# A gated convolution–MLP kernel: the gate's weights loaded as one row, and a new order of all tasks

## The chip, the cores and the metric

The kernel runs on one core of a Trainium2 chip. The metric is device time in microseconds (us); lower is better. The engines of the core are TensorE (matrix products, PE in the profile), VectorE (DVE), ScalarE (ACT), GpSimd (POOL) and SyncE (SP), which here only issues transfers (DMAs).

## The reference, cut to what matters

One token matrix x (2048 × 640, bf16) goes through two branches, and a gate per token mixes them:

```python
g = _sigmoid((x * gate_w).sum(-1, keepdims=True))
a = _A_ref(x, A_k, A_v, A_shift_k, A_ssm_k, A_ssm_D)   # q * (long convolution of (short conv of k) * v)
b = _B_ref(x, B_w1, B_w2, B_w3, B_w4)                  # layernorm, w1, gelu, token shifts, w2, layernorm, w3, gelu, w4
return g * a + (1 - g) * b
```

Branch A's long convolution (length 2048, FFT of 4096) is done with products by small trigonometric matrices in stages. `gate_w` has 640 elements; the gate needs it twice: as columns that multiply the transposed, normalised x, and as its sum (because the layernorm's mean is subtracted afterwards).

## The kernel before, in words

The work is cut into 788 tasks. `build` declares them with their reads, writes and buffers. A task runs on one engine and issues a few instructions. The order is written out by hand in `ORDER`: a list of all task numbers, with a letter where a task may run on more than one engine (`a` ACT, `v` DVE, `p` POOL). `Plan.place` walks this list with rough durations to choose PSUM banks and to decide how many products of zeros (`t.fill`) are put ahead of a TensorE task to fill its expected waits in the first microseconds. Each engine then executes its own tasks strictly in the listed order, and waits when one is not ready. So an engine can be held up by one late task although later ones are ready, and SP, which issues nearly all DMAs, holds back every transfer behind one that waits.

PSUM has 8 banks: a `w1`, `w3` or gate product takes one, most others a pair; a bank is free again when ACT or DVE has copied it out.

Task names used below (the number after the point is the token block, block group or frequency block):

- `ldx`, `ldsk`, `ldk`, `ldv`, `ldw…`: loads. `cjz`, `ldCJ`, `cjb`, `cj`: the short convolution's taps; a strip of zeros on 128 partitions (`cjz`, ACT, L488) gets the taps in its first partition (`ldCJ`, L491), a product with ones spreads them over all partitions (`cjb`, L497), and `cj` copies them out.
- `sin`, `bm`: the trigonometric table (ACT, L471) and the DMA that spreads it into the block matrix of the first FFT stage (L481).
- `st1`, `rs1`, `nm1`, `tr1`, `ev1`, `evh`: first layernorm per block: statistics (DVE or ACT), their root (POOL), normalising, transposing on TensorE (L572), copying out (L387 on DVE, L385 on ACT); `evh` makes shifted copies of two blocks.
- `trh`, `evt`, `dfold`: transposing the long kernel (L805) and copying it out.
- `w1`, `g1`, `w2`, `x1`, `sq`: first half of branch B (L647 and L651, gelu L664, L673, L680, L685); `ve2`, `st2`, `nm2`, `dt2`, `w3`, `g2`, `w4`, `t2`: its second half (L767, L774, L781/L788, L796). `dt2` is a transposing DMA (L759).
- `kv0`–`kv3`: the short convolution on DVE (L825, L829, L833).
- `s1h`, `s1hr`, `s1x`, `s1xr`, `e1…`, `wF`: first FFT stage of the kernel (h) and of kv (x) (L858, L860), copied out and written to DRAM (L890). `rF`, `s2`, `e2`, `pa`/`pb`, `s3`, `e3`, `wG`: read back (L904), second stage (L912), products (L927), way back (L940), written out (L952). `rG`, `s4`, `yq`, `ad`, `ax`, `fo`, `st`: last stage (L966, L978), gate and sum (L984, L1011, L992, L998), store.
- `ldgw`, `sgm`, `sg`, `gate`, `gz`, `gtanh`, `gg`: the gate. `ldgw` (L503) loads `gate_w` with the partition as its fastest index, so that each element goes to its own place; `sgm` (L692) sums it over partitions with a product by ones; `sg` reduces that and copies the five columns 32 times (`GB`, L697).
- `fill`: the products of zeros (L254).

TensorE tasks have a mode by the shape of their products (full, or parts of the array in rows or columns); two neighbours of different mode cost a little extra.

The order ends the kernel with the `w4` products of blocks 12 to 15 and their `fo` on DVE.

Of the kernel before, what the change touches and what calls it, by code (L numbers as in the profile page):

```python
# [16 lines left out]
P = 128  # L17
D = 640
# [13 lines left out]
FILL_US = (0.43, 0.22)  # L32
# [4 lines left out]
14 4 5 0 9 1 8 7 10 29 30 12 28 16 71v 6 17 15 31 69a 46 2 81a 3 24 27 61v 70 72 22 25a 18 23a 20 82 59v 21a 26  # L37
19a 74v 44 73v 60 87v 79v 88 11 215 75 76v 401 405 77v 84a 216 80 63a 402v 62 406a 32 83v 68p 45 403 89v 64v 43
399 400v 404v 97a 85 91v 90 65 86a 67v 42 397 398v 92a 93 94v 66a 98 100v 41 36 407 127 13 33 105v 460 95a 466
129 128 96 47 99v 461a 103v 106 464 133 50 101 102v 78p 39 467a 465a 108v 130 104 35 468 411 49 469a 462 134 131  # L40
37 48 409 448 132 463a 149 107v 38 119v 456 449a 109 457a 135 454 450 34 150 120 110a 153 410 136 40 408 157 151
455a 51 451a 412 413 452 155 121v 158 471 152 414 415 416 122 137 417 140 138 52 154 56 156 159 160 470 453a
124a 141 146 143 147 144 123a 125 126v 111a 112 472 113a 115v 114 116v 458 478 148 479a 420 473a 145 162 163 139
165 166 474 168 55 459 227 476 475a 169 117 477a 118v 421 480 422 481a 484 485a 54 142 492 171 488 172 173 177
174 175 489a 217 221 179 222 423 228 178 419 424 425 426 57 490 493a 418 225v 486 176 482 193 223a 218 427 195
180 483 487a 491a 184 194 496 219 196 185 431 231a 504 190 181 505a 497a 500 191 182 229a 501a 201 53 430 432
224 202 502 494 498 433 499a 503a 199 197 187 200 198 495 167 434 188 508 509a 516 203 226 232 428 230 204 429
435 233 517a 241 161 514 234 510 512 242 239 253 506 507 511a 164 240 513a 58 206 515a 235 254 436 437 440 520
# [35 lines left out]
class Plan:  # L84
# [62 lines left out]
    def place(self, order):  # L147
# [8 lines left out]
        for i in order:  # L156
# [33 lines left out]
            else:  # L190
                d = t.dur
                if e == "PE":
# [3 lines left out]
                    if at < WARM:  # L196
                        d *= COLD
                        if self.kept is not None:
                            t.fill = int(0.85 * (at - max(free[e], 0.8)) / FILL_US[0])
# [153 lines left out]
def build(env, nc, io):  # L353
# [19 lines left out]
    def dma(name, nbytes, fn, issue=0.58, **kw):  # L373
        return add(name, "SP", issue, fn, nbytes=nbytes, **kw)
# [679 lines left out]
```

## Time and profile before

| what | value |
|---|---|
| median of 3 runs | 228.67 us (228.23 to 228.74) |
| the profiled execution's own time | 228.84 us |
| its span in the profile | 227.1 us |
| mean granted TensorE clock | 0.992 of full |
| busy: PE, DVE, ACT, POOL | 216.0, 191.2, 156.1, 44.1 us |
| DMA | 57.25 MB, mean 252 GB/s |

The profiled execution took 1.74 us more than its span, which lies ahead of and behind the first and last instruction that the profile shows. The page's busy time of PE counts the products of zeros too (L254, 29 of them, 10.5 us), so it is not all work. The chain of waits names, from the end backwards, what released each step; shares by line tell where the kernel's time is set.

### The profile page before, as it was taken

What the parts mean: (1) busy time and instruction counts of PE and PEld (TensorE: products, weight loads), DVE (VectorE), ACT (ScalarE), POOL (GpSimd) and SP (SyncE); (2) the same over time, 40 slices, a digit from 0 to 9 for tenths busy, and PEclk for the clock granted to TensorE, in tenths of its full rate; (3) what the DMA queues carried; (4) which work ended last, traced back from release to release, by engine and by line L of the source; (5) the groups of instructions that cost most, each with busy time, mean ns of one, the idle gap of its engine ahead of it and who ended that gap; (6) DMA issues with size and microseconds to landing.
All of it is one profiled execution on the core that took longest, in us unless ns stands there. A gap on an engine that the chain in (4) does not pass through costs nothing.

```text
span 227.1 us, 5043 instructions
## 1 busy us (share of the span) xinstructions
PE 216.0 (95%) x1994; PEld 104.9 (46%) x1994; DVE 191.2 (84%) x273; ACT 156.1 (69%) x224; POOL 44.1 (19%) x91
## 2 busy tenths in 40 slices
PE   7679899999999999999999999999989999999993
PEld 2258444456445444445543333344344554545552
DVE  8988889988999999998488889798987147998982
ACT  8889899899979999979459888888965014132000
POOL 8874237730380000031330000000000000000000
PEclk9799999999999999999999999999999999999999
DMA  5899999899947899968899997989996595898632
GB/s 153 216 293 338 234 282 292 244 323 302 341 147 242 180 306 343 291 237 219 203 357 358 250 320 188 288 314 345 197 190 217 153 406 182 235 301 240 207 92 58
DMA packets 41609, 57.25 MB, mean 252 GB/s; under 512 B 15985, under 2 KB 31602, under 8 KB 41586
## 3 DMA queue, kind: packets, MB, share of 16 engines
q1 hardware_dynamic: 41266, 56.61, 84.6%
q8 instruction: 15, 0.25, 0.5%
q10 hardware_dynamic: 320, 0.33, 0.5%
q14 instruction: 8, 0.07, 0.1%
HBM read 34.90 MB, written 18.35 MB: 235 GB/s over the span
## 4 chain that ended last, share of the span: by engine, by line
PE 76%; DMA 8%; DVE 6%; ACT 5%; SPq 3%; issue 1%; DVEq 0%
PE PS L767 19%; PE PS L781 18%; PE PS L673 9%; PE PS L647 6%; PE PS L788 6%; PE PS L912 5%; PE PS L940 4%; DMA x<-in_A_q_dram 4%; DMA SK<-in_A_ssm_k_dram 3%; PE PS L858 3%; SPq L380 2%; ACT FS L385 2%; PE PS L978 2%; PE PS L651 2%; DVE VC L829 2%; DVE VC L825 2%
## 5 line engine op out<-in xcount | busy, mean ns | idle before, releaser
L774 ACT ACTIVATE h2T<-PS 128x512 bf16<-128x512 f32 x48 | 28.1, 602 | 29.4 <-PE PS L767 28.6
L781 PE MATMUL PS<-W,h2T 128*128 128x512 bf16 (+1 forms) x288 | 40.3, 299 | 0.0
L385 ACT CAST FS<-PS 128x1024 bf16<-128x1024 f32 x38 | 37.0, 1025 | 2.6 <-PE PS L860 1.6
L767 PEld LDWEIGHTS <-W 128*128 128x128 bf16 x240 | 21.3, 98 | 31.0 <-issue 9.3
L781 PEld LDWEIGHTS <-h2T 128*128 128x128 bf16 x288 | 22.2, 98 | 19.2 <-issue 1.5
L385 ACT CAST XH<-PS 128x1024 bf16<-128x1024 f32 x23 | 22.9, 1014 | 9.0 <-PE PS L912 8.0
L767 PE MATMUL PS<-x1nT,W 128*128 128x512 bf16 x120 | 28.5, 380 | 0.0
L767 PE MATMUL PS<-XB,W 128*128 128x512 bf16 x120 | 28.3, 380 | 0.0
L927 DVE TENSOR_TENSOR PP<-XH 128x2048 bf16<-128x2048 bf16 x20 | 23.6, 1221 | 1.7 <-ACT XH L385 1.0
L825 DVE TENSOR_TENSOR VC<-K,VC 128x2560 bf16<-128x2560 bf16 x16 | 23.8, 1486 | 0.2
L673 PE MATMUL PS<-W,hsT 128*128 128x512 bf16 (+1 forms) x160 | 23.4, 299 | 0.3 <-DVE x L680 0.3
L387 DVE CAST XH<-PS 128x1024 bf16<-128x1024 f32 x17 | 20.5, 1220 | 3.2 <-PE PS L912 1.5
L796 DVE TENSOR_TENSOR x<-PS,x 128x640 bf16<-128x640 f32 x12 | 9.8, 823 | 13.3 <-PE PS L781 13.3
L647 PE MATMUL PS<-xnT,W 128*128 128x512 bf16 x80 | 19.2, 379 | 0.9 <-ACT hsT L664 0.9
L673 PEld LDWEIGHTS <-hsT 128*128 128x128 bf16 x160 | 13.0, 98 | 11.8 <-issue 0.5
L829 DVE TENSOR_TENSOR VC<-VC 128x2560 bf16<-128x2560 bf16 x12 | 17.9, 1488 | 0.4
L740 POOL TENSOR_TENSOR r<-v,MH 128x2 f32<-128x2 f32 x8 | 8.2, 1021 | 50.3 <-DVE v L735 47.7
L385 ACT CAST GS<-PS 128x1024 bf16<-128x1024 f32 x15 | 14.7, 1020 | 3.8 <-PE PS L940 3.8
L984 DVE SCALAR_TENSOR_TENSOR W<-PS,GG,QO 128x640 bf16<-128x640 f32 x16 | 13.6, 878 | 3.0 <-PE PS L978 3.0
L680 DVE SCALAR_TENSOR_TENSOR x<-PS,x 128x640 bf16<-128x640 f32 x16 | 12.8, 821 | 1.0 <-PE PS L673 1.0
L788 PE MATMUL PS<-W,h2T 128*128 128x512 bf16 (+1 forms) x96 | 13.4, 299 | 0.0
L912 PE MATMUL PS<-FX,TRIG 64*32 64x512 bf16 x320 | 12.7, 382 | 0.3 <-DVE GS L387 0.3
(111 smaller groups left out, 294.8 us busy)
## 6 DMA issues: line engine op xcount, KB each, us to landing
FH<-FS SPq DMA_DIRECT2D x8, 640.0 KB, 5.4
FXD<-FS SPq DMA_DIRECT2D x8, 640.0 KB, 4.7
FX<-FH SPq DMA_DIRECT2D x10, 512.0 KB, 5.1
FX<-FXD SPq DMA_DIRECT2D x10, 512.0 KB, 5.7
GX<-GD SPq DMA_DIRECT2D x8, 640.0 KB, 5.5
W<-in_B_w_dram SPq DMA_DIRECT2D x2, 1920.0 KB
GD<-GS SPq DMA_DIRECT2D x8, 480.0 KB, 3.3
x<-in_A_q_dram SPq DMA_DIRECT2D x16, 160.0 KB, 3.4
```

Of the source, the lines that this page charges most:

```text
L385: nc.scalar.copy(out=out, in_=in_)
L387: (nc.vector if t.on == "DVE" else nc.gpsimd).tensor_copy(out=out, in_=in_)
L647: nc.tensor.matmul(m[:, b, :], lhsT=W[:, 0, kb, 160 * fb:160 * fb + 128], rhs=rhs(kb, shifts[fb]), start=(kb == 0), stop=(kb == 4))
L673: nc.tensor.matmul(m[:, c0:c1], lhsT=env["hsT"][:, o.buf["hs"][0], fb, 128 * (s % 4):128 * (s % 4) + 128], rhs=env["W12"][:, 1, fb, c0:c1] ...
L767: nc.tensor.matmul(env.PS[:, t.buf["U"][0], :], lhsT=env["W3"][:, kb, 128 * fb:128 * fb + 128], rhs=env.nT(int(nP[-1]))[:, :, kb, :], star ...
L774: nc.scalar.activation(out=env["h2T"][:, o.buf["h2"][0], fb, :], in_=env.PS[:, t.buf["U"][0], :], func=ACT.Gelu_apprx_tanh)
L781: nc.tensor.matmul(m[:, c0:c1], lhsT=env["h2T"][:, o.buf["h2"][0], fb, 128 * (s % 4):128 * (s % 4) + 128], rhs=env["W4"][:, fb, c0:c1], st ...
L788: nc.tensor.matmul(env.PS[:, t.buf["U"][0], 0:c1 - c0], lhsT=env["h2T"][:, o.buf["h2"][0], fb, 128 * (s % 4):128 * (s % 4) + 128], rhs=env ...
L825: nc.vector.tensor_tensor(out=VC[:, o], in0=env["K"][:, a + 3 - j:a + 7 - j, :], in1=w, op=ALU.mult)
L829: nc.vector.tensor_tensor(out=VC[:, 1], in0=VC[:, 1], in1=VC[:, 2], op=ALU.add)
L912: nc.tensor.matmul(env.U(t.buf["U"][0])[32 * j:32 * j + 32, gp, :], lhsT=CRI()[64 * gp:64 * gp + 64, 32 * pc:32 * pc + 32], rhs=X[64 * gp: ...
L927: nc.vector.tensor_tensor(out=env["PP"][:, o.buf["PP"][0], a, :].rearrange("p (b c) -> p b c", b=2), in0=X.unsqueeze(1).broadcast_to([P, 2 ...
```

## The change

1. `ldgw` loads `gate_w` as one row of 1,280 bytes into the first partition of the same strip of zeros that holds the taps; the strip and `cjz` grow from 2,560 to 3,200 columns.
2. A new TensorE task `gwm` multiplies five pieces of that strip by one column of ones: each product gives one column of 128 weights. A new DVE task `gwc` copies the five columns to `GW`, and 32 times to `GB`. `sg` loses its copy.
3. The rule for products of zeros in the first 7.5 planned microseconds goes from 0.85 to 0.95 of an expected wait. In the program as built there are 33 products of zeros, 29 before: 19 stand ahead of the first product with data (12 before), 14 in later waits (17 before).
4. `ORDER` is replaced as a whole: every engine's sequence is different, and some tasks change engine.

```diff
-14 4 5 0 9 1 8 7 10 29 30 12 28 16 71v 6 17 15 31 69a 46 2 81a 3 24 27 61v 70 72 22 25a 18 23a 20 82 59v 21a 26
...
+5 14 32 4 0 80p 9 1 16 31 8 6 70p 30 2 7 10 83a 73v 15 12 61v 45 17 27 3 84 81v 74 28 71a 29 18 63v 86v 33 22 11
...
-                            t.fill = int(0.85 * (at - max(free[e], 0.8)) / FILL_US[0])
+                            t.fill = int(0.95 * (at - max(free[e], 0.8)) / FILL_US[0])
...
-    add("cjz", "ACT", 2.2, lambda t: nc.scalar.copy(out=env.early("CJR", [P, 4 * D], BF16).rearrange("p (a b) -> p a b", b=512),
-                                                    in_=env.early("FZ", [P, 512], BF16).unsqueeze(1).broadcast_to([P, 5, 512])),
-        use=[zeros], w=["CJR"], roles=("C0",))
+    add("cjz", "ACT", 2.7, lambda t: nc.scalar.copy(out=env.early("CJR", [P, 5 * D], BF16).rearrange("p (a b) -> p a b", b=400),
+                                                    in_=env.early("FZ", [P, 512], BF16)[:, 0:400].unsqueeze(1).broadcast_to([P, 8, 400])),
+        use=[zeros], w=["CJR", "GWR"], roles=("C0",))
...
-    dma("ldgw", 2048, lambda t: nc.sync.dma_start(out=env.sm("GW", [P, 5], BF16)[:],
-                                                  in_=io["gw"].rearrange("(t p) -> p t", p=P)), w=["GW"])
+    dma("ldgw", 1280, lambda t: nc.sync.dma_start(out=env.early("CJR", [P, 5 * D], BF16)[0:1, 4 * D:5 * D], in_=io["gw"].unsqueeze(0)),
+        w=["GWR"], roles=("C0",))
+
+    def gwm(t):
+        row = env.early("CJR", [P, 5 * D], BF16)
+        for kb in range(5):
+            nc.tensor.matmul(env.PS[:, t.buf["U"][0], kb:kb + 1], lhsT=row[:, 4 * D + 128 * kb:4 * D + 128 * kb + 128],
+                             rhs=env["ONE"][:, 0:1], start=True, stop=True)
+    tw = add("gwm", "PE", 0.3, gwm, r=["GWR", "c0"], use=[fill], acq=[ONE], mode="f", roles=("C0",))
+
+    def gwc(t):
+        m = env.PS[:, tw.buf["U"][0], 0:5]
+        nc.vector.tensor_copy(out=env.sm("GW", [P, 5], BF16)[:], in_=m)
+        nc.vector.tensor_copy(out=env.sm("GB", [P, 5, 32], BF16)[:], in_=m.unsqueeze(2).broadcast_to([P, 5, 32]))
+    add("gwc", "DVE", 0.4, gwc, use=[tw], rel=[(tw, "U")], w=["GW"])
...
     def sg(t):
         nc.vector.reduce_sum(out=env.sm("SG", [P, 1])[:], in_=env.PS[:, ts.buf["U"][0], 0:5], axis=mybir.AxisListType.X)
-        nc.vector.tensor_copy(out=env.sm("GB", [P, 5, 32], BF16)[:], in_=env.sm("GW", [P, 5], BF16).unsqueeze(2).broadcast_to([P, 5, 32]))
-    add("sg", "DVE", 0.35, sg, use=[ts], rel=[(ts, "U")], r=["GW"], w=["SG"])
+    add("sg", "DVE", 0.2, sg, use=[ts], rel=[(ts, "U")], r=["GW"], w=["SG"])
```

The new order, as far as the prediction speaks of it:

| stretch | before | after |
|---|---|---|
| DVE up to `evh.14` | `st1` ×6, `nm1` ×5, `ev1.0`, `evh.0`, `sg`, `evt` ×3 | `st1` ×6, `gwc`, `nm1` ×4, `ev1.2`, `ev1.0`, `sg`, `evt` ×3 |
| ACT up to its first `e1h` (both with `sin` in it: before behind the four `cj`, after ahead of them) | 3 `nm1`, `ev1.2`, `ev1.14`, gelu of `w1.0.0` among others | 4 `nm1`, `evh.0`, `ev1.14`, the same gelu; otherwise the same tasks |
| PE from the first `w1` to the first `w2` | 10 `w1`, 8 `s1h`, 2 `s1hr`, `tr1.6`, `tr1.8` | 10 `w1`, 7 `s1h`, 1 `s1hr`, `tr1.4`, `tr1.6`, `tr1.8` |
| DVE up to `kv0.v` (the last of kv) | | one `nm1`, one `nm2`, `ve2.4` and `gwc` more, one `evh` less |
| SP, `bm` | 16th task, right behind `ldw1` and ahead of `ldx8` | 17th task, behind `ldw1` and `ldw2b2`, ahead of `ldx8` |
| DVE just after `kv0.v` | `ve2.4`, `x1.14`, `e1x.0`, `nm2.4` | `x1.9`, `nm2.4`, `e1x.0` |
| DVE, copies of the second FFT stage and way back (`e2`, `e3`) | 17 + 5 | 17 + 6 |
| PE, mode changes in all | 88 | 93: 2 more from the first `w2` to `s1x.0`, 1 more between `s2h.0.0` and `s3.9`, 2 more from `w3.3.0` on |
| last stage on PE | `s4.6` after three `w3.3`; `s4.14` late | `s4.3` after two `w3.3`; `s4.14` right after `s4.5` |

52 lines of the change are left out of this document (26 added, 26 removed), and 8 rows, old and new, of the table ORDER.

## The prediction

> **What bounds the kernel now.** I read the page's busy times first, then the chain of waits in order of time, then busy time by stretches of one and ten microseconds, and last the instructions in order of time around each place where the chain leaves TensorE.
>
> ```profile
> PE 216.0 (95%) x1994; PEld 104.9 (46%) x1994; DVE 191.2 (84%) x273; ACT 156.1 (69%) x224; POOL 44.1 (19%) x91
> 90.00:100.00 10.00, 9.47 (x64) 4.34 (x63) 9.72 (x11) 8.61 (x14) 0.90 (x2) 1.00 0.87 278
> 28.00:29.00 1.00, 0.38 (x2) 0.19 (x2) 0.98 (x3) 1.00 (x2) 0.79 (x2) 1.00 0.88 243
> 31.00:32.00 1.00, 0.69 (x4) 0.29 (x3) 1.00 (x3) 1.00 (x3) 0.00 (x0) 1.00 1.08 370
> 28.46 2.84 ACT L385 CAST FS<-PS 128x1024 bf16<-128x1024 f32 x3
> 28.62 1.24 PE L647 MATMUL PS<-xnT,W 128*128 128x512 bf16 x5 [0.93 <-ACT hsT L664]
> ```
>
> The columns of a stretch are PE, weight load, DVE, ACT, POOL, granted clock, DMA share and GB/s. Up to 32 us TensorE still waits while ACT is never idle (PE 0.38 and 0.69, ACT 1.00): a `w1` product waits for a bank that ACT's gelu frees (0.93 us). Behind that TensorE is nearly full; from 90 to 100 us, where the chain runs over DVE, both are (9.47 and 9.72 of 10). So a new order can win in three ways only: an earlier full TensorE at the start, fewer mode changes and waits on the way, a shorter tail. Order alone removes no product.
>
> **Part 1, the weights as a row.** The old load is issued at 6.84 us and its first user runs at 11.35.
>
> ```profile
> 6.84 0.42 SPq L503 DMA_DIRECT2D GW<-in_gate_w_dram  x1
> 11.35 0.21 PE L692 MATMUL PS<-GW,ONE 128*128 128x5 bf16 x1
> 8.00:9.00 1.00, 1.00 (x5) 0.37 (x4) 0.93 (x4) 0.97 (x3) 0.81 (x3) 0.89 0.93 307
> 9.00:10.00 1.00, 1.00 (x6) 0.39 (x4) 0.97 (x4) 1.00 (x4) 0.84 (x3) 0.50 1.03 148
> 10.00:11.00 1.00, 1.00 (x5) 0.41 (x4) 0.97 (x4) 0.51 (x1) 0.73 (x4) 0.50 0.73 137
> 0.72 3.77 SPq L380 DMA_DIRECT2D x<-in_A_q_dram  x6
> 2.01 2.33 ACT L488 COPY C<-C 128x2560 bf16<-128x2560 bf16 x1
> ```
>
> In the two microseconds before its user runs the DMAs move 148 and 137 GB/s, against 307 just ahead: some 330 KB missing, 1.1 us at 307 GB/s. I take the hole for the 640 separate elements, and it goes: every load behind it may land up to 1.1 us earlier. The Trainium skill, "DMA: Bandwidth & Descriptors", section "Rules for kernel authors", says that a load whose last dimension isn't contiguous becomes one descriptor per element; the hole agrees with that, though no row here counts them. Only loads that someone waits for turn this into time, and ACT, busy in every stretch above, waits for few; so between 0 and 1.1 us, and I take none beyond what the queue sum below brings.
>
> On SP the new load stands right behind `ldCJ`, and both wait for `cjz`. With 640 more columns `cjz` takes 2.33 × 3200/2560 = 2.91 us and ends at 4.92; SP comes there after six halves of x (4.49) and one `ldsk` of about the same 0.63 us, so at 5.1: no wait, and nothing behind it held up.
>
> The new task costs five products of one column: at most five times the 0.21 us of the similar product at 11.35, in a stretch where TensorE runs zeros anyway, so nothing; if the zeros were needed work it would be 1.05 us. `gwc` puts two small copies into DVE's early queue and `sg` gives one back: a copy of five columns, less than the 0.44 us that a `nm1` of 640 takes below; I take 0.1. `sin` now stands ahead of the `cj` on ACT, so `bm` and all loads behind it on SP are issued sooner; as long as ACT sets the pace that brings nothing by itself.
>
> **Part 2, the start, up to the first `w2`.** The first `w1` needs `evh.14`, the last of DVE's early copies.
>
> ```profile
> 16.14 1.23 DVE L387 COPY HT<-PS 128x2048 bf16<-128x2048 bf16 x1 [0.62 <-ACT xn L564]
> 20.15 2.36 DVE L387 COPY HT<-PS 128x2048 bf16<-128x2048 bf16 x2 [1.08 <-PE PS L805]
> 22.43 0.44 DVE L566 TENSOR_SCALAR xn<-x,RS,NB 128x640 bf16<-128x640 bf16 x1
> 22.78 0.88 DVE L387 COPY xnT<-PS 128x640 bf16<-128x640 bf16 x2
> 24.71 0.81 DVE L387 COPY xnT<-PS 128x1280 bf16<-128x1280 bf16 x1
> 23.93 1.24 PE L647 MATMUL PS<-xnT,W 128*128 128x512 bf16 x5
> 42.58 3.74 PE L673 MATMUL PS<-W,hsT 128*128 128x512 bf16 x24
> ```
>
> Ahead of `evh.14` DVE now has one `nm1` less (-0.44), one `ev1` more (+0.81), no `evh.0` (two copies like `evh.14`'s, -0.88) and `gwc`'s +0.1: -0.4 us. The two waits of 0.62 and 1.08 us may go as well. So the first `w1` comes 0.4 to 2.1 us before 23.93; I take 1.2, the middle. From there to the first `w2` (42.58) TensorE has one `tr1` more, one `s1h` and one `s1hr` less:
>
> ```profile
> 12.44 0.72 PE L572 MATMUL PS<-ID,xn 128*128 128x128 bf16 x10
> 33.09 0.43 PE PS L858 x2
> 30.44 0.61 PE L858 MATMUL PS<-HT,C 128*128 128x128 bf16 x8
> 17.12 1.86 ACT L385 COPY HT<-PS 128x2048 bf16<-128x2048 bf16 x1 [0.96 <-PE PS L805]
> 23.75 1.23 ACT L385 COPY xnT<-PS 128x1280 bf16<-128x1280 bf16 x1 [0.99 <-DVE xnT L387]
> 14.43 1.73 ACT L564 ACTIVATE xn<-x,NB,RS 128x640 bf16<-128x640 bf16 x2
> ```
>
> +0.72 -0.43 -0.61 = -0.3, and the 1.0 us of `s1h` comes back behind the first `w2`. Whether the lead gets through is ACT's affair. Up to its first `e1h` (28.46) ACT has the 0.58 of `cjz` and one `nm1` more (0.87), loses up to 1.95 us of the waits shown, and swaps `ev1.2` for `evh.0` at about the same (0.81 and 0.88 on DVE). First `e1h` between 0.5 earlier and 1.5 later: ACT gains little. So I let half of the lead through: -0.6 -0.3 +1.0 = **+0.1 us**, with both ends kept: the whole largest lead, -2.1 -0.3 +1.0 = -1.4; none of it and no shorter stretch, +1.0.
>
> The granted clock belongs here. It is 0.50 from 9 to 11 us (part 1), after TensorE stood idle for 1.87 us ahead of 7.86; now 19 products of zeros run up to the first product, and that gap may go.
>
> ```profile
> 7.86 1.87 PE L497 MATMUL PS<-C,ONE 128*128 128x512 bf16 x6 [1.87 <-POOL MH L414]
> 10.78 0.75 DVE L566 TENSOR_SCALAR xn<-x,RS,NB 128x640 bf16<-128x640 bf16 x2
> ```
>
> What the half clock cost: the first transposes ran at 12.44 though their blocks were normalised at 11.53, 0.9 us at most, of which the ACT-bound start passes on little; I take 0. The Trainium skill, "TensorE: Matmul & The Clock Gate", section "What's actually happening", has the array at half clock until about 3.4 us of sustained work, and back after as long a quiet; by that rule TensorE would be at full clock from about 5 us on, and the whole 0.9 could count. Here the gap was 1.87 us only, so the trace agrees with the state and not with its length.
>
> **Part 3, the hinge.** All of the second FFT stage waits for the last kv block, its first stage, and a trip through DRAM.
>
> ```profile
> 98.62 0.83 PE L860 MATMUL PS<-K,TRIG 64*128 64x512 bf16 x12 [0.25 <-DVE K L833]
> 99.73 1.52 PE L673 MATMUL PS<-W,hsT 128*128 128x512 bf16 x10 [0.28 <-DVE x L680]
> 104.92 5.75 SPq L759 DMA_TRANSPOSE XB<-xn  x3
> 110.84 0.46 SPq L904 DMA_DIRECT2D FX<-FH  x1
> 114.86 0.62 PE L912 MATMUL PS<-FX,TRIG 64*32 64x512 bf16 x16
> 115.49 1.19 PE PS L767 x5
> 120.71 2.26 PE PS L767 x10
> ```
>
> TensorE waits 0.25 us for kv at 98.62: without it it would come at 98.37. A mode change costs 0.12 us (two lone `w3` at 1.19 each against 2.26 for two in a row). So now 98.37 + 0.1 + 2 × 0.12 = 98.7. DVE's queue up to `kv0.v` grows by 0.44 (`nm1`) + 0.44 (`nm2`) + 0.3 (`ve2`, two tiny instructions, taken below one `nm1`) + 0.1 - 0.88 (`evh.0`): +0.4; less what it saves of early waits (up to 1.7 above): kv, now at 98.6, comes at 97.3 to 99.0. It is no later than TensorE but for the upper end. The first read of the second stage is issued at 110.84, right behind three transposing DMAs, and its data arrives just as TensorE gets there: no slack at all. In the new order `nm2.4` stands ahead of `e1x.0`, so its transposing DMA and all behind it on SP start earlier; I take no stall, and the 0.28 us wait for `x1` goes because `w2.14` now comes after three `s1x`: -0.28.
>
> **Part 4, the middle and the end.** One mode change more in the middle, two in the last stage: +0.36. One `e3` copy more on DVE (about 1.22 us), one less on ACT: hidden if DVE's gaps there (9.19 of 10 us busy in the fullest stretch) hold it, 1.22 if not; I take 0.
>
> ```profile
> 160.00:170.00 10.00, 9.43 (x163) 4.18 (x169) 9.19 (x9) 7.91 (x10) 0.00 (x0) 1.00 1.05 188
> PE PS L940 <- ACT GS L385: 0.6, 1, 0.6
> L387 DVE CAST GS<-PS 128x1024 bf16<-128x1024 f32 x5 | 6.1, 1223 | 1.6 <-PE PS L940 1.6
> 179.94 9.53 SPq L966 DMA_DIRECT2D GX<-GD x5
> GX<-GD SPq DMA_DIRECT2D x8, 640.0 KB, 5.5
> ```
>
> TensorE's longest wait there, 0.6 us for a copy of the way back, may go or double in a new order: 0 ± 0.6. In the last stage `s4.3` starts one `w3` (1.1 us) sooner; its read, issued at 179.94, lands about 185.4 and is early. `s4.14` now comes a `w4` and three `w3` earlier, with its read only fifth on SP, where the five issues took 9.53 us: a wait between 0 and 0.6, of which I take 0.1. The tail is the same chain: a long and a short `w4`, two `fo`, one store.
>
> **The sum.** +0.1 (start) + 0.24 (two changes) - 0.25 (kv wait, in 98.37 against 98.62) - 0.28 + 0.36 + 0.1 = +0.27 us on the profiled execution's 228.84, so 229.1; the median stands 0.17 lower: 228.67 + 0.27 = 228.9 us. Runs differ by about 0.2% (0.46 us), so this is "no change", own range 228.2 to 229.1.
>
> **The rivals.** *The start stays ACT's* (slower): with none of the lead through, the 1.0 us of postponed `s1h` is pure loss: +0.9 on the sum, 229.8 us, up to 230.4 if `cjz` and the extra `nm1` delay ACT by half a microsecond too. For it: ACT is busy 0.99 to 1.00 from 27 to 32 us. Against: ACT's two early waits. It decides from a first `w2` later than 42 us. Chance 0.22. *DVE is too full in the middle* (slower): the extra copy lands on TensorE, 228.9 + 1.2 = 230.1; for it the 9.19 of 10 above, against it the short waits. 0.13; small mishaps such as `s4.14` 0.04. *The hole in the DMAs was the brake* (faster): the largest lead gets through, -1.5 on the start, 227.4; kv must then be there by 97.3, which it just can. For it: the DMA share near 1 at 9 us; against: ACT. 0.23. *The middle's wait goes* (faster): -0.6, 228.3, with the tail of other small gains 228.0; 0.08. *The clock* (faster): the 0.9 us counts, 228.0; 0.03. That the change doesn't do what it is called is true of one part only: there are more products of zeros, not fewer, and they stand in waits.
>
> **How the numbers follow.** No change 0.27 (the likeliest single case); faster 0.23 + 0.08 + 0.03 = 0.34; slower 0.22 + 0.13 + 0.04 = 0.39. The range takes in the large rivals at their worked values (227.4, 229.8, 230.1) and 0.3 to 0.5 us beyond for the smaller terms: 227.1 to 230.6.
>
> **What would show it.** The first `w2` near 41.7 us with the GB/s near 10 us no longer halved; first kv product of the last block at 98.5 to 99; `w4` block straight into the second stage without a gap; the chain from there all TensorE. A first `w2` before 41 or after 42.3, a TensorE gap ahead of the second stage, or DVE as releaser in the middle for over a microsecond would make it wrong.

## The result, and the profile after

| | before | after |
|---|---|---|
| median (lowest to highest) | 228.67 us (228.23 to 228.91) | 230.67 us (230.34 to 231.03) |
| ratio, 95% interval | | 1.0086 (1.0063 to 1.0109) |
| profiled execution: own time, span | 228.84, 227.1 | 230.88, 229.1 |

The change makes the kernel 2.0 us slower; 228.9 was forecast, and the range ended at 230.6. The page of the changed kernel still shows TensorE full:

```profile
PE 218.7 (95%) x2003; PEld 106.4 (46%) x2003; DVE 193.4 (84%) x274; ACT 155.3 (68%) x224; POOL 42.4 (19%) x91
```

So the question is when TensorE and ACT get into their stride. Six places in the order of time answer it. After (start, duration, engine, line, instruction, wait in brackets):

```profile
25.99 1.24 PE L660 MATMUL PS<-xnT,W 128*128 128x512 bf16 x5
29.82 0.60 ACT L677 ACTIVATE hsT<-PS 128x512 bf16<-128x512 f32 x1
43.98 4.24 PE L686 MATMUL PS<-W,hsT 128*128 128x512 bf16 x30
101.16 0.82 PE L872 MATMUL PS<-K,TRIG 64*128 64x512 bf16 x6 [0.30 <-DVE K L845]
103.93 13.21 PE L793 MATMUL PS<-W,h2T 128*128 128x512 bf16 x96
117.07 0.62 PE L924 MATMUL PS<-FX,TRIG 64*32 64x512 bf16 x16
```

and of before, the one mark that the prediction does not show, the first gelu:

```profile
27.97 0.60 ACT L664 ACTIVATE hsT<-PS 128x512 bf16<-128x512 f32 x1
```

The first `w1` comes 2.06 us later (25.99 against 23.93) and the first gelu 1.85 us later. From the gelu to the end there are 199.3 us against 199.1. Nearly all of the loss lies in the first 30 us, though the whole order was replaced. There the first difference is on POOL and DVE. Before:

```profile
2.45 3.51 POOL L477 MEMSET C<- 128x4096 bf16 x1
5.27 0.89 DVE L447 TENSOR_SCALAR PRE<-C 128x32 int32<-128x32 int32 x2
5.68 0.48 DVE L449 SCALAR_TENSOR_TENSOR PRE<-C 128x160 int32<-128x160 int32 x1
7.58 0.68 DVE L545 BATCH_NORM_STATS2 BS<-x 128x6 f32<-128x512 bf16 x1
```

and after:

```profile
2.81 1.71 POOL L407 TENSOR_SCALAR_AFFINE_SELECT ID<-ID 128x128 bf16<-128x128 bf16 x1
4.47 3.51 POOL L477 MEMSET C<- 128x4096 bf16 x1
5.22 2.95 DVE L447 TENSOR_SCALAR PRE<-C 128x32 int32<-128x32 int32 x2
5.63 2.54 DVE L449 SCALAR_TENSOR_TENSOR PRE<-C 128x160 int32<-128x160 int32 x1
9.49 0.69 DVE L558 BATCH_NORM_STATS2 BS<-x 128x6 f32<-128x512 bf16 x1
```

POOL now makes the identity matrix (`ident`, L406 and L407) ahead of the memset `bz` (L477), which ends at 7.98 instead of 5.96 us. Two small operations of DVE's `phsmall` begin at the same time as before and end 0.2 us behind the memset in both kernels, at 6.16 and at 8.17. So what the profile shows as a long duration is, by these ends, a wait. DVE's statistics start 1.9 us late. Next comes TensorE:

```profile
12.72 0.32 DVE L516 CAST GB<-PS 128x160 bf16<-128x160 f32 x1
13.09 0.17 PE L705 MATMUL PS<-GW,ONE 128*128 128x5 bf16 x1 [2.12 <-DVE GB L516]
14.39 1.92 PE L817 MATMUL PS<-ID,SK 128*128 128x128 bf16 x16
16.10 1.27 PE L585 MATMUL PS<-ID,xn 128*128 128x128 bf16 x10
```

```profile
13.00:14.00 1.00, 0.91 (x5) 0.38 (x5) 0.96 (x5) 0.12 (x1) 0.81 (x3) 0.91 0.84 245
14.00:15.00 1.00, 1.00 (x8) 0.74 (x7) 1.00 (x4) 1.00 (x2) 0.84 (x3) 0.50 0.62 177
15.00:16.00 1.00, 1.00 (x13) 1.00 (x11) 0.97 (x4) 0.97 (x4) 0.73 (x4) 0.50 0.94 365
16.00:17.00 1.00, 1.00 (x12) 1.00 (x11) 0.17 (x2) 0.92 (x3) 0.82 (x3) 0.50 1.01 385
17.00:18.00 1.00, 1.00 (x17) 1.00 (x15) 0.53 (x1) 1.00 (x2) 0.81 (x3) 0.88 1.00 384
```

`sgm` is early in the new PE order and needs `gwc`, which stands on DVE behind three late `st1`. PE waits 2.12 us, and behind that wait the granted clock (third number from the end) is 0.50, from 13.8 to 17.2 us if the shares at both ends are worked out: `trh.1` takes 1.92 us where 1.16 is usual, `tr1.2` 1.27 instead of 0.72. The last late piece is ACT's; SP also stands, for `cjb.2`:

```profile
22.67 1.28 ACT L385 COPY xnT<-PS 128x640 bf16<-128x640 bf16 x2 [2.37 <-DVE xnT L387]
28.53 1.28 ACT L677 ACT_TABLE_LOAD   x1
```

```profile
SPq L481 <- PE PS L497: 6.5, 1, 6.5
```

These are five suspects: the memset (A), PE's stand for `gwc` (B) with the clock behind it (E), SP's stand (C), `evh.0` on ACT (D). The first gelu follows 7.15 us behind the start of `evh.0`, with ACT never idle between; the last 1.28 us of them are a table that ACT loads ahead of the gelu.

### The profile page after: what moved, and what is told of

Same layout as the page of the kernel before. It is cut to its first block, busy times and chain, and to the rows that moved or that the text cites. A ratio compares the mean times of both kernels' runs of the same rounds, so it can differ in the third digit from the quotient of the medians.

```text
span 229.1 us, 5061 instructions
## 1 busy us (share of the span) xinstructions
PE 218.7 (95%) x2003; PEld 106.4 (46%) x2003; DVE 193.4 (84%) x274; ACT 155.3 (68%) x224; POOL 42.4 (19%) x91
## 4 chain that ended last, share of the span: by engine, by line
PE 74%; DVE 13%; ACT 5%; issue 2%; SPq 2%; DMA 1%; DVEq 0%; ACTq 0%
PE PS L779 18%; PE PS L793 17%; PE PS L686 8%; PE PS L660 7%; PE PS L924 5%; PE PS L952 4%; PE PS L800 4%; PE PS L870 3%; DVE VC L837 3%; DVE VC L841 3%; PE PS L990 2%; SPq L380 2%; PE PS L664 1%; DMA x<-in_A_q_dram 1%; DVE K L845 1%
## 5 line engine op out<-in xcount | busy, mean ns | idle before, releaser
L786 ACT ACTIVATE h2T<-PS 128x512 bf16<-128x512 f32 x48 | 27.6, 605 | 25.7 <-PE PS L779 25.4
L779 PE MATMUL PS<-XB,W 128*128 128x512 bf16 x120 | 29.0, 381 | 0.0
L385 ACT CAST GS<-PS 128x1024 bf16<-128x1024 f32 x14 | 13.9, 1015 | 5.2 <-PE PS L952 5.2
L752 POOL TENSOR_TENSOR r<-v,MH 128x2 f32<-128x2 f32 x8 | 6.8, 856 | 48.8 <-DVE v L747 48.8
L254 PE MATMUL PS<-C 128*128 128x512 bf16 x33 | 11.5, 496 | 1.2 <-DVE C L484 1.2
```

The source lines that it names most:

```text
L385: nc.scalar.copy(out=out, in_=in_)
L779: nc.tensor.matmul(env.PS[:, t.buf["U"][0], :], lhsT=env["W3"][:, kb, 128 * fb:128 * fb + 128], rhs=env.nT(int(nP[-1]))[:, :, kb, :], star ...
L786: nc.scalar.activation(out=env["h2T"][:, o.buf["h2"][0], fb, :], in_=env.PS[:, t.buf["U"][0], :], func=ACT.Gelu_apprx_tanh)
```

## The experiments

All kernels start from the changed kernel unless the text says otherwise, with the counts of products of zeros held to its own; diffs show the order of one engine's tasks by name. Kernels that were timed together share runs of the kernel before, and each ratio is to those runs. The last three columns are from each kernel's profiled execution; the last one is worked out from its unrounded span.

| kernel | median us | ratio to before, 95% | first `w1` | first gelu | span less first gelu |
|---|---|---|---|---|---|
| before | 228.67 | 1 | 23.93 | 27.97 | 199.1 |
| after | 230.67 | 1.0086 (1.0063 to 1.0109) | 25.99 | 29.82 | 199.3 |
| e5 row alone, order before | 228.41 | 1.0000 (0.9983 to 1.0017) | 23.56 | 27.61 | 199.1 |
| e6 `bz` late, order before | 228.94 | 1.0014 (1.0000 to 1.0028) | 23.87 | 28.03 | 199.2 |
| e1 `bz` early | 228.39 | 1.0000 (0.9973 to 1.0027) | 24.99 | 28.81 | 199.3 |
| e2 `sgm` later | 229.74 | 1.0067 (1.0045 to 1.0088) | 24.66 | 28.50 | 199.3 |
| e3 `cjb.2` earlier | 232.40 | 1.0159 (1.0135 to 1.0183) | 27.37 | 31.19 | 199.3 |
| e10 more zeros | 229.83 | 1.0073 (1.0042 to 1.0104) | 24.81 | 28.65 | 199.3 |
| e7 `bz` early, row late | 229.52 | 1.0041 (1.0028 to 1.0054) | 24.61 | 28.45 | 199.3 |
| e11 e7, more zeros | 228.92 | 1.0005 (0.9982 to 1.0029) | 23.34 | 27.17 | 199.3 |
| e12 e1, more zeros | 228.89 | 1.0007 (0.9983 to 1.0031) | 24.09 | 27.92 | 199.3 |
| e13 e12, row loads first | 228.89 | 0.9998 (0.9977 to 1.0019) | 23.96 | 27.80 | 199.3 |
| e8 e7, `evh.0` on DVE | 229.86 | 1.0050 (1.0030 to 1.0069) | 24.48 | 28.53 | 199.7 |
| e9 `evh.0` on DVE | 231.26 | 1.0118 (1.0102 to 1.0133) | 25.72 | 29.85 | 199.5 |
| e14 e11, `st1.4` later | 228.87 | 1.0010 (0.9983 to 1.0037) | 23.53 | 27.87 | 199.3 |
| e15 `st1.4` later | 230.74 | 1.0092 (1.0074 to 1.0111) | 25.32 | 29.66 | 199.3 |
| e16 `bz` early, `st1.4` later | 228.68 | 0.9994 (0.9973 to 1.0015) | 25.02 | 29.36 | 199.3 |
| e17 e14, `sin` later, zeros moved | 228.27 | 1.0001 (0.9970 to 1.0033) | 22.62 | 26.50 | 199.3 |
| e19 `st1.4` later, `evt.4` earlier | 230.25 | 1.0055 (1.0035 to 1.0076) | 25.78 | 29.29 | 199.3 |
| e18 e17, `evt.4` earlier | 228.26 | 0.9976 (0.9951 to 1.0002) | 22.22 | 26.04 | 199.3 |

The last column is the main finding: whatever is moved in the start, 199.3 us follow the first gelu in the new order, and 199.1 or 199.2 in the old one; only the two kernels with `evh.0` on DVE stray (199.7 and 199.5), for a reason that stays open. The executions of six kernels with an early `bz` (e1, e11, e14, e16, e17, e18) spread over 2.1 to 3.4 us, so their medians say less than their traces, and a trace is one execution. But every execution has its mean granted clock on record. In the traces 0.991 to 0.993 goes with 3.4 us of half clock in the start, 0.983 to 0.985 with 6.8 us, and 0.998 to 1.000 with none.

**e5, the first part of the change alone, in the order before.**

```diff
 PE:  cjb.3,
+     gwm,
      cjb.2
 DVE: st1.14,
+     gwc,
      nm1.1
 sg:
-     copy of the columns to GB
```

> The kernel before in its own order and with its own counts of products of zeros, with the first part of the change alone: the gate's weights loaded as one row, `gwm` on PE ahead of `cjb.2` and `gwc` on DVE behind `st1.14`, and the broadcast of the columns out of `sg`. Theory (the loss lies in the new order, not in the row): the time is within 0.2% of the kernel before, 228.3 to 229.1 us, with the first `w1` at 23.7 to 24.3 us. Rival (the row itself costs, by 5 more products and a PE wait, or by the later columns): 229.3 us or more, with the first `w1` over 0.5 us later than 23.93. On the gap in the loads at 9 to 11 us (148 and 137 GB/s before): if the load of 640 single elements made it, it goes here; if not, it stays within 20%.

```profile
9.00:10.00 1.00, 0.73 (x4) 0.12 (x1) 0.97 (x4) 1.00 (x3) 0.73 (x4) 0.50 1.07 310
10.00:11.00 1.00, 0.62 (x7) 0.35 (x8) 0.97 (x5) 1.00 (x2) 0.82 (x3) 0.50 0.80 303
```

228.41 us: the row is free, and the loss lies in the order. The gap in the loads is gone (310 and 303 GB/s for 148 and 137; e6 below, which keeps the old load, still has it with 141 and 173), and nothing is gained by it. The changed kernel has a gap of its own at 10 us (137 GB/s), so its trace alone would have misled.

**e1, the memset early.**

```diff
 POOL: iota, evz.0, iotb,
+      bz,
       evz.14, ident,
-      bz,
       ones
```

> The changed kernel with one POOL task moved: the memset `bz` (3.51 us) runs right behind `iotb`, as in the kernel before, instead of behind `ident`; the products of zeros are pinned to the changed kernel's counts. Theory A (the memset makes the small phase operations of DVE wait): L447 and L449 end at about 6.2 us instead of 8.2, DVE's first st1 starts at about 7.6 us instead of 9.49, `gwc` ends near 11.1 instead of 13.04 and `sgm` follows at once; the first `w1` comes 0.8 to 1.9 us earlier than 25.99, and the time is 228.8 to 229.9 us. Rival (the two us of DVE are hidden, the start hangs on ACT's copies and on the `ssm_k` loads): st1 is earlier by the same 1.9 us, but the first `w1` stays within 0.3 us of 25.99 and the time is 230.4 to 230.8 us.

```profile
5.23 1.01 DVE L447 TENSOR_SCALAR PRE<-C 128x32 int32<-128x32 int32 x2
7.67 0.68 DVE L558 BATCH_NORM_STATS2 BS<-x 128x6 f32<-128x512 bf16 x1
10.98 0.27 PE L509 MATMUL PS<-ONE,C 128*128 128x1 bf16 x5 [4.10 <-DMA C<-in_gate_w_dram]
28.81 0.60 ACT L677 ACTIVATE hsT<-PS 128x512 bf16<-128x512 f32 x1
```

228.39 us, against 228.50 of the kernel before in the same runs: moving one task gives back the whole loss, somewhat more than theory A had set. DVE does as forecast (statistics at 7.67). The profiled execution took 229.86 us and gains 1.0 us only: in it the row landed at 10.98 instead of 8.90 us, and PE stood 4.1 us for it. The six executions at 227.8 to 228.1 have no trace, but their mean granted clock is 0.997 to 1.000, while it is 0.985 to 0.993 in five of the other six (the sixth took 229.86 us at 1.000). So the half clock goes with most of the difference between the quick and the long executions.

**e6, the same move the other way round, in the order before.**

```diff
 POOL: iota, iotb,
-      bz,
       ident,
+      bz,
       ones
```

> The kernel before with one POOL task moved: `bz` runs behind `ident`, as in the changed kernel; nothing else. Theory A (the order of POOL's first tasks makes the loss, in either order of the rest): L447 and L449 end 0.2 us behind the end of `bz`, near 8.1 us instead of 6.16, the first st1 starts near 9.5 instead of 7.58, and of these 1.9 us the start's own waits (0.62 and 1.08 us of DVE, 1.66 us of PE for the `ssm_k` load) take up a part: first `w1` 0.4 to 1.9 us later than 23.93 and the time 229.0 to 230.4 us. Rival (the order before has room for it, only the new order is held up): first `w1` within 0.3 us of 23.93 and the time within 0.2% of the kernel before.

```profile
5.26 2.95 DVE L446 TENSOR_SCALAR PRE<-C 128x32 int32<-128x32 int32 x2
5.67 2.54 DVE L448 SCALAR_TENSOR_TENSOR PRE<-C 128x160 int32<-128x160 int32 x1
9.53 0.69 DVE L544 BATCH_NORM_STATS2 BS<-x 128x6 f32<-128x512 bf16 x1
```

DVE is held in the same way (2.95 us, statistics at 9.53), yet the time is within 0.2%: the rival was right. The order before has room for 1.9 us of DVE; the new one has not. `gwc` and `sgm` in its early chain are one reason, but not the whole: with `sgm` out of the way (e2, next) 1.24 of the 2.0 us stay, and PE waits 0.91 us for DVE's normalising ahead of `tr1.2`.

**e2, `sgm` behind `tr1.2`, and e10, the stand filled with zeros.**

```diff
 PE (e2):  cjb.1,
-          sgm,
           cjb.0, trh.1, tr1.2,
+          sgm,
           trh.2
 (e10): products of zeros ahead of sgm
-          3
+          12
```

> The changed kernel with one PE task moved: `sgm` runs behind `tr1.2` instead of ahead of `cjb.0`, so that PE no longer stands 2.12 us for `gwc`; the products of zeros are pinned. Theory B (this stand is on the path, with the drop of the granted clock behind it): `cjb.0` starts near 11.0 us instead of 13.12, `trh.1` near 12 instead of 14.39 and at 1.2 us instead of 1.92, `tr1.2` near 14.8 instead of 16.1, the first `w1` 0.5 to 1.3 us earlier than 25.99, and the time is 229.5 to 230.2 us. Rival (PE only waits elsewhere: DVE's `nm1` or ACT's `evh.0` come last): the first `w1` moves by less than 0.3 us and the time is 230.4 to 230.8 us.

> The changed kernel with 12 products of zeros ahead of `sgm` instead of 3, and nothing moved: they fill the 2.12 us in which PE stands for `gwc`. Theory E (what costs is not the stand but the granted clock of 0.50 behind it, at which `trh.1` took 1.92 instead of 1.17 us and `tr1.2` 1.27 instead of 0.72): the clock stays at 1.0 from 11 to 18 us, `sgm` still comes at 13.1, `trh.1` and `tr1.2` take 1.16 and 0.72 us, the first `w1` comes 1.0 to 1.3 us earlier than 25.99, and the time is 229.4 to 229.8 us. Theory A (DVE's late chain sets the first `w1`, PE has room): clock and durations the same, but the first `w1` within 0.4 us of 25.99, 230.3 to 230.8 us.

The trace of e10, PE in the order of time and one stretch:

```profile
13.45 0.17 PE L705 MATMUL PS<-GW,ONE 128*128 128x5 bf16 x1
14.47 1.15 PE L817 MATMUL PS<-ID,SK 128*128 128x128 bf16 x16
15.46 0.72 PE L585 MATMUL PS<-ID,xn 128*128 128x128 bf16 x10
28.65 0.60 ACT L677 ACTIVATE hsT<-PS 128x512 bf16<-128x512 f32 x1
```

```profile
14.00:15.00 1.00, 1.00 (x13) 0.81 (x12) 1.00 (x4) 0.77 (x2) 0.84 (x3) 1.00 0.74 293
```

In e10 `sgm` comes even 0.36 us later, but the clock stays at 1.00, `trh.1` takes 1.15 and `tr1.2` 0.72 us, and the first gelu comes 1.17 us earlier: theory E. The medians stand 1.17 (e10) and 1.24 us (e2) above those of the kernel before in the same runs, where the changed kernel stood 2.00: a gain of about 0.8 us each, of the 1.17 and 1.32 that the gelu gained. The intervals of all three ratios overlap, so the size is less certain than the mechanism. That the clock stayed up is not the luck of one trace: nine of e10's twelve executions have a mean clock of 0.998 or more, and all five of the changed kernel 0.985 to 0.993.

**e3, `cjb.2` ahead of `trh.1`.**

```diff
 PE:  cjb.0,
+     cjb.2,
      trh.1, tr1.2, trh.2,
-     cjb.2
 ACT: cj.1,
+     cj.2,
      st1.6, nm1.0, nm1.15,
-     cj.2
```

> The changed kernel with `cjb.2` moved on PE from behind `trh.2` to ahead of `trh.1`, and its copy `cj.2` on ACT to behind `cj.1`, so that SP's `bm`, which stood 6.5 us for `cjb.2`, is issued earlier; the products of zeros are pinned. Theory C (the late loads behind `bm` cost time): `bm` is issued near 14.5 us instead of 19.66, the loads behind it 4 to 5 us earlier, and the time is 229.6 to 230.4 us. Rival (these loads have slack: no first wait for a load of `x` or `k` is seen in the changed kernel between 26 and 100 us): `bm` is as much earlier, the first `w1` and the first product of kv move by less than 0.3 us, and the time is 230.4 to 230.9 us.

`bm` is issued at 15.76 instead of 19.66 us, and the time is 1.7 us longer. Theory C falls: span less first gelu is 199.3 with `bm` 3.9 us earlier. The loss is of the edit's own making (`trh.1` only at 16.32 and at half clock, `evh.0` 1.37 us later), so the rival's "same" was wrong too.

**e7, row late, and e11, the same with more zeros.**

```diff
 both: bz early as in e1
 PE:  trh.1,
+     gwm,
      tr1.2, trh.2,
+     sgm
 DVE: nm1.1,
+     gwc,
      ev1.2, evt.1, evt.2,
+     sg
 zeros ahead of cjb.3, trh.1:
-     19, 2   (e7)
+     26, 10  (e11)
```

> The changed kernel with `bz` right behind `iotb` and with the gate's row taken off the start of the chain: `gwm` on PE behind `trh.1`, `gwc` on DVE where `sg` stood, `sgm` behind `trh.2`, `sg` behind `evt.2`; the 19 products of zeros stand ahead of `cjb.3`, the 3 of `sgm` go. If PE's waits for the row's load and for `gwc` still cost beside the early `bz`: first `w1` at 22.4 to 23.0 us and the time 227.0 to 227.9 us. If DVE and ACT end last without them: first `w1` near 23 to 24 us, as in the quick executions of the kernel with `bz` moved alone, 227.8 to 228.6 us. Behind the first `w1` every trace so far has 203.1 us to the end, and so should this one.

> The kernel with `bz` early and the row's products late, with more products of zeros: 26 ahead of `cjb.3` (19) and 10 ahead of `trh.1` (2), where PE stood 1.1 and 1.66 us and the clock fell to 0.50. Theory E: `trh.1` takes 1.16 us instead of 1.86 and `tr1.2` 0.72 instead of 1.12, the first `w1` comes at 23.2 to 23.7 us instead of 24.61, and the time is 227.9 to 228.6 us instead of 229.52. Rival (ACT's `nm1.0`, `nm1.15` or `evh.0` come last): first `w1` within 0.3 us of 24.61, 229.2 to 229.7 us.

e7, then e11:

```profile
12.58 1.86 PE L817 MATMUL PS<-ID,SK 128*128 128x128 bf16 x16 [1.66 <-ACT VC L385]
14.80 1.12 PE L585 MATMUL PS<-ID,xn 128*128 128x128 bf16 x10
28.45 0.60 ACT L677 ACTIVATE hsT<-PS 128x512 bf16<-128x512 f32 x1
```

```profile
12.58 1.16 PE L817 MATMUL PS<-ID,SK 128*128 128x128 bf16 x16
13.91 0.72 PE L585 MATMUL PS<-ID,xn 128*128 128x128 bf16 x10
27.17 0.60 ACT L677 ACTIVATE hsT<-PS 128x512 bf16<-128x512 f32 x1
```

e7 missed both expectations: with the row out of the way PE stands for `cj.3`, and the clock falls again. With eight more zeros there, and seven more ahead of `cjb.3`, `trh.1`, at the same 12.58, takes 0.70 us less and the gelu comes 1.28 us earlier. That is theory E a second time: first `w1` as expected, and the gelu 0.8 us ahead of the kernel before. The median, 228.92, is above what was expected, with executions from 228.2 to 230.3.

**e12 and e13: more zeros on e1; then both row loads ahead of `ldsk1`.**

```diff
 zeros ahead of gwm, sgm, trh.1:
-     19, 3, 2
+     28, 4, 6
 SP (e13): ldx14,
+     ldCJ, ldgw,
      ldsk1,
-     ldCJ, ldgw
```

> The changed kernel with `bz` right behind `iotb` and more products of zeros: 28 ahead of `gwm` (19), 4 ahead of `sgm` (3), 6 ahead of `trh.1` (2). With `bz` moved alone, half of the executions took 227.8 to 228.1 us and half 229.4 to 230.0; in the profiled one of the second kind PE stood 4.1 us for the load of the row and the clock was 0.50 from 11 to 14 us. Theory E (the clock parts these two kinds): the second kind goes, all executions at 227.6 to 228.3 us, first `w1` at 22.8 to 23.2 us. Rival (the late row itself parts them): both kinds stay, median 228.2 to 229.0 us.

> The kernel above with the two row loads `ldCJ` and `ldgw` issued ahead of the 512 KB load `ldsk1` instead of behind it. If the late landing of the row holds up the start: `gwm` starts near 8.0 us or earlier in every execution, first `w1` at 22.6 to 23.0 us, 227.4 to 228.0 us, the best of all kernels here. Rival (`ldsk1`, issued 0.6 us later, then holds up `trh.1`): `trh.1` up to 0.6 us later than in the kernel above, and the time 0 to 0.6 us more.

Neither theory came out: 228.89 us both, in e12 within its rival's range. The executions lie closer (228.4 to 229.9), but the zeros themselves now hold `gwm` until 9.73 and 9.61 us. In all 24 executions the mean clock is 0.998 or more, so the half clock is gone from the start, and the 1.1 to 1.5 us over which they still spread are not its doing. How much of e1's spread is the row's landing stays open.

**e8 and e9, `evh.0` on DVE, on e7 and on the changed kernel.**

```diff
 ACT:
-     evh.0,
      st1.7, ev1.14
 DVE: ev1.0,
+     evh.0,
      evt.3, evh.14
```

> The kernel above (row late, `bz` early) with `evh.0` on DVE behind `ev1.0`, as in the order before, instead of on ACT, where it stood 2.2 to 2.4 us for `ev1.0` and made `trh.4` wait 1.0 us. Theory D: `trh.4` 0.6 us earlier, ACT's `st1.7`, `ev1.14` and `evt.4` 1 us earlier, first `w1` 0.4 to 1.0 us earlier than in the kernel above, and the time as much less. Rival (DVE has then 0.8 us more to do ahead of `evt.3` and `evh.14`, and the first `w1` waits for `evh.14`): first `w1` within 0.3 us, the same time or 0.3 us more.

> The changed kernel with `evh.0` on DVE behind `ev1.0` and nothing else; products of zeros pinned. It tells how much of the 2.0 us this move alone made. Theory D: first `w1` 0.4 to 1.0 us earlier than 25.99, 229.6 to 230.3 us. Theory A (all of the loss is the late `bz` and what waits behind it): first `w1` within 0.3 us of 25.99, 230.4 to 230.9 us.

Theory D isn't borne out. The first `w1` is 0.13 and 0.27 us earlier, the first gelu is not (28.53 for 28.45, 29.85 for 29.82), and the times are longer. ACT, freed of `evh.0`, waits 2.58 and 3.19 us for DVE's `evh.14` ahead of `ev1.14`. The comparison isn't clean: the half clock lasts from 11.3 to 18.1 us in e8's trace and from 11.2 to 18.0 in e9's, longer than in the kernels that they start from, and `trh.2` takes 1.91 instead of 1.17 us in e8 and 1.48 instead of 1.19 in e9.

**e14, e15, e16: `st1.4` behind `evt.3`, on e11, on the changed kernel, and on e1.**

```diff
 DVE: ev1.2, evt.1, evt.2,
-     st1.4,
      nm1.14, ev1.0, evt.3,
+     st1.4,
      evh.14
```

> The kernel with `bz` early, the row's products late and more products of zeros, and on DVE `st1.4` moved from ahead of `nm1.14` and `ev1.0` to behind `evt.3`. In five traces of the new order the first `w1` comes 9.35 to 9.45 us behind the start of `tr1.2` wherever the clock is full. Theory F (these 9.4 us are DVE's: `ev1.2`, `evt.1`, `evt.2`, `st1.4`, `nm1.14`, `ev1.0`, then ACT's `evh.0` and `trh.4`, `trh.0`): without the 1.05 us of `st1.4` in it, 8.3 to 8.6 us, first `w1` 22.3 to 22.7 us instead of 23.34, and the time 0.7 to 1.0 us under the kernel it starts from, 227.3 to 228.2 us. Rival (PE with its 9 products of zeros, 2.6 us, sets them): still 9.3 us, no change over 0.2 us. Behind the first `w1` 203.1 us as in the other traces, unless the later statistics hold up a transpose there.

> The changed kernel with `st1.4` on DVE moved to behind `evt.3` and nothing else; products of zeros pinned. Theory F: `tr1.2` at 16.1 us as before, first `w1` 0.8 to 1.1 us earlier than 25.99, 229.6 to 230.0 us. Rival (PE's zeros): first `w1` within 0.2 us of 25.99, 230.5 to 230.9 us.

> The changed kernel with the two smallest moves together: `bz` right behind `iotb` on POOL, `st1.4` behind `evt.3` on DVE; products of zeros pinned. If the two gains add (2.3 us for `bz` alone, 0.8 to 1.1 by theory F): 227.2 to 228.0 us, faster than the kernel before. If the row's late landing in some executions spoils it as with `bz` alone: two kinds again, near 227 and near 228.8.

e15:

```profile
21.67 1.28 ACT L385 COPY xnT<-PS 128x640 bf16<-128x640 bf16 x2 [1.37 <-DVE xnT L387]
25.32 1.02 PE L660 MATMUL PS<-xnT,W 128*128 128x512 bf16 x4 [0.15 <-DVE xnT L387]
29.66 0.60 ACT L677 ACTIVATE hsT<-PS 128x512 bf16<-128x512 f32 x1
```

`evh.0` starts 1.0 us earlier and the first `w1` 0.67, but the gelu only 0.16, and the time is the same (230.74). So the chain up to `ev1.0` is DVE's, as theory F has it, and the first `w1` is not what the time counts from. e14 and e16 gain nothing either, but their traces differ in the start as well (in e14 the zeros hold the first `cjb` until 9.62 us, 8.72 in e11; in e16 the half clock falls on `trh.1`, which takes 1.91 us, 1.16 in e1), so they add nothing to that.

**e17: `sin` behind the three `cj`.**

```diff
 ACT: st1.0,
-     sin,
      cj.3, cj.0, cj.1,
+     sin,
      st1.6
```

> The first kernel of this set with `sin` on ACT moved from ahead of `cj.3` to behind `cj.1`, 2 products of zeros ahead of `trh.1` and 5 ahead of `tr1.2`. If `cj.3` behind the 2.17 us of `sin` is what holds `trh.1` at 12.58 us: `trh.1` near 10.7, `tr1.2` near 13.0 (then by DVE's `nm1`), first `w1` 0.6 to 1.0 us earlier than in that kernel, 226.5 to 227.6 us. If the `ssm_k` load holds it (its landing isn't seen): `trh.1` stays near 12.5 us and the time within 0.3 us; `bm` is then up to 2 us later, which cost nothing so far.

`trh.1` starts at 10.86 instead of 12.58 us (e7, e11), `tr1.2` at 13.05 instead of 13.91 (e11): ACT's `cj.3` behind `sin` had held it, not the load. First gelu 26.50, the profiled execution 227.54 us. The median is 228.27, with executions from 227.4 to 230.7.

**e19 and e18: `evt.4` ahead of `ev1.14`, on e15 and on e17.**

```diff
 ACT: st1.7,
+     evt.4,
      ev1.14,
-     evt.4,
      g1.0.0
```

> The changed kernel with `st1.4` on DVE behind `evt.3` and `evt.4` on ACT ahead of `ev1.14`; nothing else, products of zeros pinned. `st1.4` alone made the first `w1` 0.67 us earlier, the first `s1h` only 0.16 us, and the time no shorter. Theory G (both must come earlier): `evt.4` ends before 27.0 us instead of 28.34, the first `s1h` at 28.1 to 28.3 instead of 28.91, the time 229.9 to 230.2 us. Rival (what ACT does behind the first `s1h` counts: `ev1.14` is only put off and the gelus come no earlier): the first `s1h` earlier, but the end less than 0.3 us, 230.4 to 230.8 us.

> The kernel with `bz` early, row late, `st1.4` and `sin` moved, and on ACT `evt.4` moved ahead of `ev1.14`. In thirteen of fifteen traces of the new order the end comes 200.0 us behind the first `s1h`, which needs `evt.4` through `dfold`. Theory G (the first `s1h`, by ACT's `evt.4` or by PE's two `w1` ahead of it, is what the time counts from): `evt.4` 1 us earlier than 23.32, the first `s1h` then by PE alone, 0.2 to 0.3 us earlier than 25.76, and the time 0.2 us under the kernel it starts from, 226.8 to 228.1 us. Rival (the gelus behind it on ACT count, which do not move): no change of the span over 0.1 us, 227.1 to 228.4 us.

In e19 the end comes 199.7 us behind the first `s1h`, elsewhere 200.0, while 199.3 us behind the first gelu is the common value: the gelu is the mark, and theory G is right only in that `evt.4` had to move as well. With it moved, ACT has 7.15 us without a pause from `evh.0` to the gelu, as in the changed kernel (7.99 in e15, with a pause for `evh.14`); `evh.0` itself is 0.5 us later than in e15 in this trace, `trh.2` having run at half clock, and 230.25 us is just above what was expected. That trace has 6.8 us of half clock, e15's 3.4; e19's three executions with a mean clock of 0.993 took 229.3 to 229.9 us, e15's four with 0.990 to 0.992 took 230.7. In e18 the first `s1h` comes 0.47 us earlier than in e17 (25.29 for 25.76) and the gelu 0.46, so that run doesn't part the two marks. e18:

```profile
18.89 1.28 ACT L385 COPY xnT<-PS 128x640 bf16<-128x640 bf16 x2 [1.08 <-DVE xnT L387]
26.04 0.60 ACT L677 ACTIVATE hsT<-PS 128x512 bf16<-128x512 f32 x1
```

e18, with e17 (228.27) the fastest here, takes 228.26 us: 2.4 us under the changed kernel, and with 0.9976 (0.9951 to 1.0002) not shown to beat the kernel before.

## Why the prediction was wrong

The forecast sum can be set against the four stretches of the two traces (starts taken from the rows above and those of the prediction):

| stretch | forecast | measured |
|---|---|---|
| up to ACT's first gelu: the lead let through | -0.6 | 27.97 to 29.82: +1.85 |
| to the first product of the last kv block: `tr1`, postponed `s1h`, two mode changes, kv wait | -0.3 +1.0 +0.24 -0.25 = +0.69 | 70.65 to 71.34: +0.69 |
| to the second FFT stage: the `x1` wait | -0.28 | 16.24 to 15.91: -0.33 |
| to the end: three mode changes, `s4.14` | +0.46 | 112.2 to 112.0: -0.2 |
| sum | +0.27 | +2.0 |

**Part 1 held in the order before.** There the row costs nothing, the hole of 148 and 137 GB/s was the load of 640 elements, and its end brings no time (e5). That speaks against the rival "the hole in the DMAs was the brake". Part 1's reason, that ACT is busy in every stretch shown, misreads the row from 10 to 11 us (0.51), but nothing hung on it. In the new order the new products cost more than the nothing of Part 1: PE stands for the row, 0.58 us in the changed kernel's trace and 1.5 to 4.1 us in e1, e2, e3, e9, e10, e16 and e19.

**Part 2 failed, in the step "so the first `w1` comes 0.4 to 2.1 us before 23.93".** It came 2.06 us after that mark, at 25.99. The step added up DVE's tasks ahead of `evh.14` and took them to start when they did before. It did not look at the order on POOL, where the memset had moved beside `phsmall` (1.9 us), nor at the new PE wait that the change adds: `sgm` behind `gwc`, with `cjb.0`, `trh.1` and all transposes queued behind it. Each has its run: e1 for the first, e2 and e10 for the second. Against the kernel before in the same runs, e1 takes back all of the 2.0 us and e2 and e10 about 0.8 each; the two overlap, since `gwc` is late because the statistics ahead of it are. In single traces the lead was there to be had: with both out of the way and more zeros the first `w1` comes at 23.34 (e11) and, with `sin` and `st1.4` moved too, at 22.62 us (e17). The medians don't show it: no ratio lies clear below that of the kernel before.

**The clock was priced at 0, and only as a possible gain.** As a gain, 0 was right. The kernel before has the half clock too, from 8.8 to 12.2 us, where the `cjb` products lie: of its 130 executions timed beside the experiments, the 102 with a mean clock of 0.989 to 0.993 have a median of 228.6 us, and the 15 with 0.997 or more one of 228.7. As a loss it was left out. The new order has it where the chain runs: behind PE's stand of 2.12 us `trh.1` and `tr1.2` ran at 0.50, and without that the first gelu comes 1.17 us earlier (e10). The Trainium skill, "TensorE: Matmul & The Clock Gate", section "What's actually happening", asks for about 3.4 us of quiet before the half clock. Here the clock fell behind stands of 2.12 (after) and 1.34 us (e15) for `gwc`, and within one of 1.66 us in e7; but in e10 PE stood 2.28 us for the row with no fall behind it. In e3, e9 and e19 the clock was down from 11.2 to 11.4 us on, ahead of the stand for `gwc` or within its first half microsecond; there PE had stood 1.67 to 2.35 us for the row before. So 3.4 us are not needed here, and the length of a stand alone does not decide.

**Parts 3 and 4.** The hinge came out as summed, partly by luck: the 0.28 us wait for `x1` went as forecast, but the wait for kv stayed (0.30 for 0.25). The two pieces of the stretch ahead of it were 0.15 us shorter each than summed (from the gelu to the first `w2` 14.16 us after and 14.61 before, -0.45 for -0.3; from there to the kv product +1.14 for +0.99, with the kv wait that stayed in it), and why was not followed up. Behind the second stage one wait of 0.33 us went and the longest stayed,

```profile
171.42 1.39 PE L952 MATMUL PS<-PP,TRIG 32*64 32x512 bf16 x32 [0.55 <-ACT GS L385]
```

so that the stretch is 0.2 us shorter and not 0.46 longer; what hides the mode changes there was not tried.

**The rivals.** "The start stays ACT's" gave the nearest time (229.8 to 230.4) and its sign, a first `w2` later than 42 us, was seen (43.98). ACT's first gelu is indeed what the time counts from. But its mechanism, an ACT too busy to pass the lead on, is not what happened: ACT stood 1.35, 0.95 and 2.37 us for PE and DVE, and there was no lead.

## What to carry to other kernels

When a whole order is replaced, walk the first microseconds of every engine, the nearly idle one too: one task moved on POOL, 19% busy, held DVE for 1.9 us, and DVE held PE. Look for the mark behind which all versions take the same time (here ACT's first gelu) and price each edit by what it does to that mark. By these runs an in-order engine should not meet a product that nobody needs soon (`sgm`, whose gate runs at 68.8 us) ahead of its critical work, and a wait there is worth filling, since the clock behind it cost 1.2 to 1.3 us here (e10, e11).

## What the runs showed of the hardware

A memset of POOL makes some DVE operations wait for its end, and DVE operations make some of POOL's wait; the profile shows it as duration. Held were `TENSOR_SCALAR` 128x32 int32 (two together 0.89 us before, 2.95 after and in e6), not the `TENSOR_SCALAR` of one element per partition (0.13 to 0.16 us in both) nor `TENSOR_TENSOR` 128x1024 (1.22 us beside the memset before, two in 2.30 after, ahead of it). The other way round, `AFFINE_SELECT` took 1.71 us beside that `TENSOR_TENSOR` and 0.29 in the kernel before, where it starts behind it. The Trainium skill, "SBUF — State Buffer", section "Who interferes with whom", has one port pair shared by DVE and GpSimd as an exclusive lock, held for the whole instruction, by `tensor_scalar` in its two-port mode against any GpSimd operation and by two-input operations only against one that reads SBUF; all these rows agree.

The half clock comes in steps: in the twelve traces where it falls in the start, it lasts 3.4 us in seven (in the rows of the changed kernel above the clock lost is 0.09, three times 0.50, and 0.12 us, which at half clock makes 3.4) and 6.8 us in five (e3, e5, e8, e9, e19), whatever the length of the stand ahead of it.

SP also has waits that the profile puts down to a transfer's landing and that no task of the order names. In e1 it stood 1.6 us for `ldsk1` before it issued `ldsk2` at 10.26 us, and the loads fell to 92 GB/s from 10 to 11 us:

```profile
SPq L533 <- DMA SK<-in_A_ssm_k_dram: 1.6, 1, 1.6
```

```profile
10.00:11.00 1.00, 0.02 (x1) 0.05 (x2) 0.92 (x3) 1.00 (x1) 0.65 (x2) 0.95 0.36 92
```
